# Two weight loads of a fused recurrence and expert kernel, moved and cut into other pieces

## The chip, the core and the metric

The kernel runs on one core of one Trainium2 chip. The metric is the device time of one execution in microseconds; smaller is better. The core has engines with instruction queues of their own: TensorE (PE, with its weight loads PEld), VectorE (DVE), ScalarE (ACT), GpSimd (POOL) and SyncE (SP). SP issues nearly all the transfers, in order; POOL issues the gathers and scatters by index. The transfers of both run on the same 16 DMA engines.

## The reference

Two stages follow each other. The first is a recurrence over 768 time steps for 4 batches and 8 heads of 48 channels:

```python
for t in range(S):
    cur = einsum('bhd,bhe->bhde', u * k[t], v[t])
    y[t] = einsum('bhd,bhde->bhe', r[t], state + cur)
    state = w[t][..., None] * state + einsum('bhd,bhe->bhde', k[t], v[t])
```

Its output, as 3072 tokens of 384 values, goes to a layer of 8 experts. A token whose product with `w_skip` is not positive is left as it is. The others go to the expert with the largest gate:

```python
h = maximum(x[mask] @ w1[e], 0)            # w1: 384 x 1024
out[mask] = x[mask] + gate[mask] * (h @ w2[e])   # w2: 1024 x 384
```

## The kernel before, in words

**The recurrence.** The work is cut into 24 chunks of 128 time steps (all heads of a batch at a time). The program's loop over `s` runs from -2 to 24. In step `s` it loads chunk `s + 4`, prepares chunk `s + 2` (two scans on DVE, lines 309 and 331, with the products `rk`, `kq` and `rp` on POOL), makes the scores and masks of chunk `s + 1` (`psA` on PE, `asb` on DVE), finishes chunk `s` (`outputs`, `evict`, `rows_out`), and stores chunk `s - 1` to `out` (line 435). So step `s` begins on DVE with the scan of chunk `s + 2`: step 5 at 37.88 us, step 12 at 73.22, step 16 at 94.47, step 21 at 121.09. The order on PE, ACT, DVE and POOL is as the program is written.

**The router.** After every six chunks a router runs, spread in small pieces over the following steps: gates, ranks, and marks (`hot`, on POOL, ACT or DVE). After the last six it gives the indices `idr`, by which POOL gathers the tokens of the experts (line 442). An early part of expert 0 (`early_expert`, 128 tokens, gathered by line 609) fills PE while the last router runs.

**The experts.** Matmuls of the experts 1 to 7 use split weights: a high part (an ACT copy to float32r) and a low part (raw less high). `w12` has both weights of an expert; `load_weights(e, q)` brings one of them (q = 0 the first, q = 1 the second; 1.5 MB) into a raw buffer. There are two raw buffers. `r0` takes (0, 0) and all later first weights but expert 1's; `r1` takes (0, 1), then (1, 0), then (1, 1), then the second weights of the others. A new load into a buffer waits for the last reader of what was in it. Expert 0's first weights are used raw. A weight is split in six slices of 512 columns, numbered 0 to 5 for the first weights and 6 to 11 for the second:

- `split_high(e, i)` (lines 101 to 108) makes the high part on ACT and puts the low part, a subtraction on POOL (line 107), on the list `low_parts`, which is run in the next step behind that step's `prep_reads`.
- `split_slice(e, i)` makes the high part on ACT (line 88) and the low part on DVE (line 89).

Before, (0, 1) is loaded in steps 5, 6 and 7, (1, 0) in 16, 17 and 18, (0, 0) in 19, 20 and 21, one transfer of 512 KB each. `parts` is the list of slices for `split_high`: expert 0's slices 6 to 11 from step 7 on, in steps in which no marks are waiting (7, 8, 12, 13, 14 and 15), expert 1's slice 0 in step 18 and its slices 1 to 5 from step 22 on, two per step.

**Behind the recurrence.** A loop runs the last router with pieces of `early_expert` between. Then come the rest of `early_expert`, `early_tokens(1)` (the next tokens of expert 0, transposed to `xT0[1]`), the gates and the indices `ids`, and `load_weights(1, 1)`, held back until the first gather has landed. Then `expert(e)` runs for all experts. In its loop over `q` it makes the hidden values `psH`, their high part `hh` (ACT) and low part `hl` (DVE), and one slice of the next expert's weights; then `tokens(e + 1)` makes `xTh` and `xTl`, then the outputs `psO` are made and scattered. `expert(0)` splits slices 6 to 11 of expert 1: those of `load_weights(1, 1)`.

Of the kernel before, what the change touches and what calls it, by code (L numbers as in the profile page):

```python
# [20 lines left out]
E, DM, DF = 8, 384, 1024  # L21
# [7 lines left out]
KC = DM // P  # L29
# [6 lines left out]
NHB = 11  # L36
HEAD = 7
STEP = 214
W_AT = 4
RW = 2112  # L40
R_OFF = 1 + NP * CW
K_OFF = R_OFF + NP * P
# [14 lines left out]
def rwkv_moe_kernel(ctx, tc, wrk, wrk0, vN, uP, wgs, wgp, w12, cst, out):  # L57
    nc = tc.nc
# [13 lines left out]
    def wtile(e, k):  # L72
        nm = f"{WN[k]}{e % 2}"
        pool = wset0 if nm in ("w1h1", "w1l1", "w2h0", "w2l0") else wset1[0]
        t = wsp[e, k] = pool.tile([P, KC * DF], F32R, tag=nm, name=f"{nm}_{e}")
        return t

    def load_weights(e, q):
        m = 1 if e == 1 else q
        wr = wset0.tile([P, KC * DF], F32, tag=f"r{m}", name=f"r{m}_{e}{q}")  # L80
        raws[e, q] = wr
        for i in range(3):
            o = i * 1024
            yield nc.sync.dma_start(wr[:, o:o + 1024],
                                    w12[e, :, q * KC * DF + o:q * KC * DF + o + 1024])

    def split(dst_h, dst_l, src, eng=None):
        nc.scalar.copy(dst_h, src)  # L88
        (eng or nc.vector).tensor_tensor(dst_l, src, dst_h.bitcast(F32), op=ALU.subtract)  # L89

    def split_slice(e, i, eng=None):
        q, cs = i // 6, slice((i % 6) * 512, (i % 6 + 1) * 512)
        for k in (2 * q, 2 * q + 1):
            if (e, k) not in wsp:
                wtile(e, k)
        split(wsp[e, 2 * q][:, cs], wsp[e, 2 * q + 1][:, cs], raws[e, q][:, cs], eng)
# [3 lines left out]
    def split_high(e, i):  # L100
        q, cs = i // 6, slice((i % 6) * 512, (i % 6 + 1) * 512)
        for k in (2 * q, 2 * q + 1):
            if (e, k) not in wsp:
                wtile(e, k)
        hi, lo, raw = wsp[e, 2 * q][:, cs], wsp[e, 2 * q + 1][:, cs], raws[e, q][:, cs]
        nc.scalar.copy(hi, raw)
        low_parts.append(lambda: nc.gpsimd.tensor_tensor(lo, raw, hi.bitcast(F32),
                                                         op=ALU.subtract))
# [31 lines left out]
    with tc.tile_pool(name="att", bufs=2) as att, \  # L140
# [141 lines left out]
        later, held, marks, ending = deque(), [], deque(), []  # L282
# [14 lines left out]
        work, lgs, gens = {}, {}, {}  # L297
# [327 lines left out]
        def early_tokens(j):  # L625
            ps = ps1.tile([P, KC, P], F32, tag="psT", name=f"psX0{j}", bufs=2)
            for kc in range(KC):
                nc.tensor.transpose(ps[:, kc], xg[j][:, kc * P:(kc + 1) * P], ident)
            nc.scalar.copy(xT0[j], ps)
# [3 lines left out]
        def early_low(k):  # L633
            while hfs and k > 0:
                dst, hf, hh = hfs.pop(0)
                nc.vector.tensor_tensor(dst, hf, hh, op=ALU.subtract)
                k -= 1
# [25 lines left out]
        def fill(k):  # L663
            psw = ps1.tile([P, 512], F32, tag="psT", name="psw", bufs=2)
            for _ in range(k):
                nc.tensor.matmul(psw, warm[:, :P], warm, start=True, stop=True)

        with tc.manual_schedule():
            setup()
            fill(FILL0)  # L670
            parts = [(4, 0, i) for i in range(6, 12)] + [(15, 1, 0)] + [(19, 1, i) for i in range(1, 6)]
            for s in range(-2, n + 1):
                on = lambda i: 0 <= i < n
                if s == -1:
                    for o in range(2):
                        for g in range(2):
                            at = 2 * (g ^ o)
                            nc.sync.dma_start(wgp_half[half(o), g, :, 2 * D:],
                                              wgp[half(g), at:at + 2, 2 * D:])
                if s + 4 < n:  # L680
                    load_chunk(s + 4)
                if on(s + 3) and s + 3 >= 1:
                    load_turned(s + 3)
                    load_v(s + 3)
                if s == 1:
                    nc.sync.dma_start(c_sb[:, C_IOTA:], cst[:, C_IOTA:])
                if s == LATE:
                    nc.sync.dma_start(wgs_sb, wgs)
                if on(s - 1):
                    store(s - 1)  # L690
                marked = len(marks)
                if pace[0] == 1:
                    mark_some()
                for i0, m in GROUPS:
                    if i0 + m == s:
                        pace[0] = 1 if i0 + m < LATE else 2
                        later.append(router(i0, m))
                        if i0 + m == LATE:
                            later.append(early())
                if on(s):  # L700
                    update(s)
                    if s == 0:
                        fill(3)
                if on(s + 2):
                    prep_scan(s + 2)
                drip(pace[0])
                if on(s):
                    outputs(s)
                if on(s + 2):
                    prep_keys(s + 2)  # L710
                    drip(pace[0])
                    prep_reads(s + 2)
                while low_parts:
                    low_parts.pop()()
                if s == -2:
                    bonus_keys(0)
                    nc.gpsimd.memset(vt_sb[3], 0.0)
                    nc.gpsimd.memset(onesb, 1.0)
                    nc.gpsimd.memset(ohs, 0.0)
                    nc.gpsimd.memset(key, 0.5)  # L720
                if on(s):
                    evict(s)
                    carry(s)
                if on(s + 1):
                    scores(s + 1)
                    bonus_sums(s + 1)
                    rows_of_keys(s + 1)
                    if s == -1:
                        fill(4)
                    flush()  # L730
                    mask(s + 1, 0)
                    mask(s + 1, 1)
                    bonus(s + 1)
                    drip(3 * pace[0])
                if on(s + 2):
                    prep_check(s + 2)
                if s == n - 1:
                    early_tokens(0)
                if on(s):
                    rows_out(s)  # L740
                flush(False)
                if pace[0] > 1:
                    mark_some(3)
                if s in (1, 2, 3):
                    nc.scalar.copy(*((trib, tri), (identb, ident),
                                     (iota, c_sb[:, C_IOTA:C_IOTA + 2 * P]))[s - 1])
                if s == 4:
                    nc.scalar.copy(toks_ps[:, :GROUPS[-1][1], :, 0], tok[:, GROUPS[-1][0]:])
                k = s + 1 - W_AT
                for eq, k0 in (((0, 1), 2), ((1, 0), 13), ((0, 0), 16)):  # L750
                    if k == k0:
                        gens[eq] = load_weights(*eq)
                    if k0 <= k < k0 + 3:
                        next(gens[eq])
                for _ in range(1 if s < 22 else 2):
                    if parts and k >= parts[0][0] and (not marked or s == 15):
                        split_high(*parts.pop(0)[1:])

        for p in parts:
            split_high(*p[1:])  # L760
        while low_parts:
            low_parts.pop()()
        while len(later) > 1:
# [5 lines left out]
        with tc.manual_schedule(engines={nc.tensor.engine, nc.scalar.engine, nc.vector.engine}):  # L769
            todo, due, done = early_expert(), HEAD * STEP, [0]  # L770
            while later:
                drip()
                flush()
                due += STEP
                while due > 0:
                    due -= next(todo, 1 << 20)
                    done[0] += 1
            early_low(1)
            for k in range(done[0], 6 * FC - 4):
                next(todo)  # L780
            early_tokens(1)
            ending.pop()()
            nc.vector.tensor_reduce(gates, pt[:, :, 2:].rearrange("p j q e -> p j e q"),
                                    axis=AX, op=ALU.add)
            nc.vector.tensor_scalar(idf, gates, 0.0, BIG, op0=ALU.is_equal, op1=ALU.mult)
            nc.vector.tensor_tensor(ids, idf, idr, op=ALU.add)
            drain(todo)
            held_back(load_weights(1, 1), gathered[0])
# [309 lines left out]
```

## Time and profile before

| | us |
|---|---|
| median of 3 runs | 287.21 |
| lowest and highest run | 287.07, 288.65 |
| the profiled execution | 286.06 |
| its span, first to last instruction | 284.2 |
| PE busy | 271.2 |
| DVE busy | 217.0 |
| ACT busy | 159.4 |
| POOL busy | 145.9 |

Busy time is the time in which an engine executes; the span is what the trace shows. The difference between the profiled execution's own time and its span, 1.86 us, lies around the instructions. All busy figures are sums over stages with different limits, and the rows further below go by stage.

### The profile page before, as it was taken

Reading aid. Unit: us, or ns where it says so; the run is one execution under the profiler, and the core shown is the slowest. Engines: PE = TensorE matmul, PEld = TensorE weight load, DVE = VectorE, ACT = ScalarE, POOL = GpSimd, SP = SyncE. Lnnn points to the kernel's source line nnn. Section 1 sums busy time; section 2 is a strip of 40 time slices with the busy share of each in tenths; the row PEclk is TensorE's granted clock in tenths of the full one; section 3 lists DMA queues with packets and bytes.
Section 4 is the critical chain, followed back from the end, with each engine's and each line's share of the span. In section 5 each row is a group of like instructions: output and inputs, shape, how many; then the busy total and the mean of one; then the engine's idle time right before and its main releaser. Section 6 shows DMA issues by size and latency. Waiting matters only on the chain.

```text
span 284.2 us, 8967 instructions
## 1 busy us (share of the span) xinstructions
PE 271.2 (95%) x3601; PEld 248.9 (88%) x3602; DVE 217.0 (76%) x414; ACT 159.4 (56%) x464; POOL 145.9 (51%) x140
## 2 busy tenths in 40 slices
PE   6998999999999999999999999999999999999993
PEld 2687878788887888887999999999999999999992
DVE  7997999999989999972747697948859588595320
ACT  5175555787658957768416573827638276381310
POOL 4986775699978998974656625011030110201111
PEclk9999999999999999999999999999999999999999
DMA  7999999998999869992078997565672656700001
GB/s 217 239 311 333 277 345 339 363 332 246 297 278 302 252 218 348 308 310 65 28 256 294 345 314 267 212 213 200 221 258 68 231 200 221 268 5 28 10 5 41
DMA packets 26131, 64.41 MB, mean 227 GB/s; under 512 B 4342, under 2 KB 15386, under 8 KB 26080
## 3 DMA queue, kind: packets, MB, share of 16 engines
q1 hardware_dynamic: 23712, 58.14, 62.3%
q0 software_dynamic: 2048, 5.48, 5.9%
q8 instruction: 30, 0.49, 0.7%
q10 hardware_dynamic: 320, 0.13, 0.2%
q14 instruction: 21, 0.17, 0.2%
HBM read 56.69 MB, written 7.86 MB: 227 GB/s over the span
## 4 chain that ended last, share of the span: by engine, by line
PE 57%; POOL 8%; issue 6%; DVE 4%; ACT 3%; DMA 1%; POOLq 0%; DVEq 0%; ACTq 0%
PE psH L884 7%; PE psH L883 7%; PE psH L882 7%; PE psO L906 6%; PE psO L908 6%; PE psO L907 6%; PE psH L133 4%; PE psY L409 3%; POOL rp L336 2%; PE psA L358 2%; POOL kq L326 2%; PE psY L413 2%; PE psX L815 2%; PE psO L658 2%; PE psX L425 1%
## 5 line engine op out<-in xcount | busy, mean ns | idle before, releaser
L820 POOL DMA_INDIRECT out<-fin,ids x16 | 16.8, 1047 | 99.1 <-DVE fin L915 92.7
L889 ACT ACTIVATE hh<-psH 128x256 fp32r<-128x256 f32 x60 | 23.1, 385 | 56.6 <-PE psH L884 53.4
L884 PE MATMUL psH<-xTh,w1l 128*128 128x256 f32 x168 | 47.5, 283 | 0.0
L883 PE MATMUL psH<-xTl,w1h 128*128 128x256 f32 x168 | 47.5, 283 | 0.0
L882 PE MATMUL psH<-xTh,w1h 128*128 128x256 f32 x168 | 47.5, 283 | 0.0
L906 PE MATMUL psO<-w2h,hh 128*128 128x384 f32 x120 | 40.9, 341 | 0.0
L908 PE MATMUL psO<-w2h,hl 128*128 128x384 f32 x120 | 40.2, 335 | 0.0
L907 PE MATMUL psO<-w2l,hh 128*128 128x384 f32 x120 | 40.1, 335 | 0.0
L894 DVE SCALAR_TENSOR_TENSOR hl<-psH,hh 128x256 fp32r<-128x256 f32 x60 | 25.1, 418 | 13.3 <-ACT hh L889 12.0
L326 POOL TENSOR_TENSOR kq<-wrk,q 128x512 f32<-128x512 f32 x24 | 28.2, 1177 | 11.7 <-DVE q L309 3.5
L364 DVE TENSOR_TENSOR asb<-psA,c_sb 128x512 f32<-128x512 f32 x48 | 30.4, 676 | 3.5 <-PE psA L358 3.4
L331 DVE TENSOR_TENSOR_SCAN rh<-wrk,rowsk,pss 128x520 f32<-128x520 f32 x24 | 31.1, 1296 | 2.0
L318 POOL TENSOR_TENSOR rk<-wrk 128x512 f32<-128x512 f32 x24 | 31.0, 1292 | 2.4 <-DMA wrk<-wrk 2.4
L884 PEld LDWEIGHTS psH<-xTh,w1l 128*128 128x128 f32 x168 | 32.2, 192 | 0.0
L883 PEld LDWEIGHTS psH<-xTl,w1h 128*128 128x128 f32 x168 | 32.2, 192 | 0.0
L882 PEld LDWEIGHTS psH<-xTh,w1h 128*128 128x128 f32 x168 | 32.2, 191 | 0.0
L309 DVE TENSOR_TENSOR_SCAN q<-wrk,pss 128x520 f32<-128x520 f32 x24 | 29.5, 1230 | 3.0 <-DMA wrk<-wrk 0.9
L336 POOL TENSOR_TENSOR rp<-wrk,rh 128x512 f32<-128x512 f32 x23 | 27.2, 1181 | 5.4 <-DVE rh L331 5.0
L89 DVE TENSOR_TENSOR w2l<-r,w2h 128x512 fp32r<-128x512 f32 x42 | 27.7, 685 | 2.0 <-ACT w2h L88 1.4
L409 PE MATMUL psY<-asb,v 128*48 128x128 f32 x384 | 26.5, 276 | 2.6 <-DVE psY L381 2.3
L915 DVE SCALAR_TENSOR_TENSOR fin<-psO,gates,xg 128x384 f32<-128x384 f32 x15 | 9.3, 618 | 25.2 <-PE psO L908 24.6
L358 PE MATMUL psA<-rp,kq 64*64 64x128 f32 (+1 forms) x768 | 26.0, 251 | 1.8 <-issue 1.1
(154 smaller groups left out, 608.4 us busy)
## 6 DMA issues: line engine op xcount, KB each, us to landing
r<-w SPq DMA_DIRECT2D x48, 512.0 KB
wrk<-wrk SPq DMA_DIRECT2D x21, 772.5 KB
v<-vN SPq DMA_DIRECT2D x24, 192.0 KB
vt<-wrk SPq DMA_DIRECT2D x48, 96.0 KB
out<-x SPq DMA_DIRECT2D x24, 192.0 KB
wrk<-wrk SPq DMA_DIRECT2D x1, 579.4 KB
wrk<-wrk SPq DMA_DIRECT2D x1, 512.0 KB
wrk<-wrk SPq DMA_DIRECT2D x1, 384.0 KB
```

Of the source, the lines that this page charges most:

```text
L318: nc.gpsimd.tensor_tensor(work[i]["rk"].rearrange("p a j -> p (a j)"), t[:, R_OFF:K_OFF], t[:, K_OFF:V_OFF], op=ALU.mult)
L326: nc.gpsimd.tensor_tensor(kq, wk["k"], wk["q"][:, :, 1:1 + P], op=ALU.mult)
L331: nc.vector.tensor_tensor_scan(rh.rearrange("p a j -> p (a j)"), wk["w"][:, 0:NP * CW], reads_at[:, :NP * CW], rowsk, op0=ALU.mult, op1=AL ...
L336: eng.tensor_tensor(rp, wk["r"], rh[:, :, :P], op=ALU.mult)
L358: nc.tensor.matmul(psa[g][j:j + HP, a, j:], wk["kq"][rows, a, j:j + HP], wk["rp"][rows, a, j:], start=True, stop=True)
L409: nc.tensor.matmul(y_at(a, g), v[:, 2 * a + g], wk["asb"][g][:, a], start=False, stop=True, skip_group_check=True)
L882: nc.tensor.matmul(ps, w1h[:, o:o + P], xTh[:, kc], start=(kc == 0), stop=False)
L883: nc.tensor.matmul(ps, w1h[:, o:o + P], xTl[:, kc], start=False, stop=False)
L884: nc.tensor.matmul(ps, w1l[:, o:o + P], xTh[:, kc], start=False, stop=(kc == KC - 1))
L906: nc.tensor.matmul(pso, h[j, fc][0], w2h[:, o], start=(fc == 0), stop=False)
L907: nc.tensor.matmul(pso, h[j, fc][0], w2l[:, o], start=False, stop=False)
L908: nc.tensor.matmul(pso, h[j, fc][1], w2h[:, o], start=False, stop=(fc == FC - 1))
```

## The change

`load_weights` makes six transfers of 256 KB (512 columns) instead of three of 512 KB, for every load of weights. A table `fetch` gives the step of each: (0, 1) one piece each in steps 5, 6, 8, 9, 13 and 15; (0, 0) two each in 19, 20 and 21; (1, 0) two each in 22, 23 and 24. A table `parts` gives the step of each `split_high`: expert 0's slices 6 to 11 in steps 7, 11, 12, 13, 18 and 21. Expert 1's slices 0 to 5 are no longer in it: they are split by `split_slice`, three ahead of the rest of `early_expert` and three behind `early_tokens(1)`. Both low parts of `early_expert` are made ahead of them.

```diff
-        for i in range(3):
-            o = i * 1024
-            yield nc.sync.dma_start(wr[:, o:o + 1024],
-                                    w12[e, :, q * KC * DF + o:q * KC * DF + o + 1024])
+        for i in range(6):
+            o = i * 512
+            yield nc.sync.dma_start(wr[:, o:o + 512],
+                                    w12[e, :, q * KC * DF + o:q * KC * DF + o + 512])
...
-            parts = [(4, 0, i) for i in range(6, 12)] + [(15, 1, 0)] + [(19, 1, i) for i in range(1, 6)]
+            fetch = {5: (0, 1), 6: (0, 1), 8: (0, 1), 9: (0, 1), 13: (0, 1), 15: (0, 1)}
+            fetch.update({t: (0, 0) for t in (19, 20, 21)})
+            fetch.update({t: (1, 0) for t in (22, 23, 24)})
+            parts = {t: 6 + i for i, t in enumerate((7, 11, 12, 13, 18, 21))}
...
-                k = s + 1 - W_AT
-                for eq, k0 in (((0, 1), 2), ((1, 0), 13), ((0, 0), 16)):
-                    if k == k0:
+                if s in fetch:
+                    eq = fetch[s]
+                    if eq not in gens:
                         gens[eq] = load_weights(*eq)
-                    if k0 <= k < k0 + 3:
+                    for _ in range(1 if eq == (0, 1) else 2):
                         next(gens[eq])
-                for _ in range(1 if s < 22 else 2):
-                    if parts and k >= parts[0][0] and (not marked or s == 15):
-                        split_high(*parts.pop(0)[1:])
-
-        for p in parts:
-            split_high(*p[1:])
+                if s in parts:
+                    split_high(0, parts[s])
...
-            early_low(1)
+            early_low(2)
+            for i in range(3):
+                split_slice(1, i)
             for k in range(done[0], 6 * FC - 4):
                 next(todo)
             early_tokens(1)
+            for i in range(3, 6):
+                split_slice(1, i)
             ending.pop()()
```

## Rows read from the trace of the kernel before

**Rows 1.** Windows: stretch, its length, busy us (x instructions) per engine, clock, DMA.

```profile
core 0: us, PE busy (x) PEld busy (x) DVE busy (x) ACT busy (x) POOL busy (x), PEclk, DMA share, GB/s
...
41.00:126.00 85.00, 81.78 (x1733) 70.90 (x1729) 80.67 (x149) 60.74 (x213) 74.84 (x67) 1.00 0.95 300
126.00:135.00 9.00, 8.36 (x145) 6.83 (x141) 2.40 (x9) 5.93 (x17) 4.14 (x5) 1.00 0.32 109
135.00:151.50 16.50, 16.49 (x157) 16.02 (x156) 10.12 (x34) 6.31 (x18) 9.78 (x9) 1.00 0.47 166
151.50:280.00 128.50, 127.83 (x909) 127.22 (x907) 87.41 (x174) 65.15 (x147) 25.91 (x24) 1.00 0.52 182
```

**Rows 2.** Timeline of DVE, steps 7 to 20: start, length, instruction, [idle before <-releaser].

```profile
54.10 1.24 DVE L309 TENSOR_TENSOR_SCAN q<-wrk,pss 128x520 f32<-128x520 f32 x1 [0.41 <-ACT gall L505]
...
106.64 1.29 DVE L331 TENSOR_TENSOR_SCAN rh<-wrk,rowsk,pss 128x520 f32<-128x520 f32 x1
107.85 1.26 DVE L364 TENSOR_TENSOR asb<-psA,c_sb 128x512 f32<-128x512 f32 x2
...
115.82 1.24 DVE L309 TENSOR_TENSOR_SCAN q<-wrk,pss 128x520 f32<-128x520 f32 x1 [0.17 <-ACT gall L505]
```

**Rows 3.** Timeline of POOL, steps 13, 17 and behind the recurrence.

```profile
80.69 1.18 POOL L326 TENSOR_TENSOR kq<-wrk,q 128x512 f32<-128x512 f32 x1 [1.37 <-DVE oh L476]
...
100.28 1.27 POOL L107 TENSOR_TENSOR w2l<-r,w2h 128x512 fp32r<-128x512 f32 x1
...
127.15 1.25 POOL L609 DMA_INDIRECT xg<-out,id  x1 [0.85 <-DMA r<-w]
...
140.57 1.02 POOL L442 DMA_INDIRECT xg<-out,idr  x1 [2.05 <-DVE pss L495]
```

**Rows 4.** Timeline of PE behind the recurrence.

```profile
134.33 2.42 PE L133 MATMUL psH<-xT,r 128*128 128x128 f32 x20
...
144.38 0.49 PE L628 MATMUL psX<-c_sb,xg 128*128 128x128 f32 x3
...
151.78 0.42 PE L906 MATMUL psO<-w2h,hh 128*128 128x384 f32 x1
...
156.15 0.28 PE L883 MATMUL psH<-xTl,w1h 128*128 128x256 f32 x1
```

**Rows 5.** Groups of instructions, the splits: busy us, mean ns of one.

```profile
L89 DVE TENSOR_TENSOR w1l<-r,w1h 128x512 fp32r<-128x512 f32 x36 | 24.9, 691 | 1.8 <-issue 0.2
...
L88 ACT CAST w1h<-r 128x512 fp32r<-128x512 f32 x36 | 22.2, 615 | 0.0
...
L107 POOL TENSOR_TENSOR w1l<-r,w1h 128x512 fp32r<-128x512 f32 x6 | 7.5, 1266 | 3.9 <-ACT lgs L432 3.3 <-ACT w1h L106 0.6
```

**Rows 6.** Timeline of SP's queue: transfers issued.

```profile
101.58 0.33 SPq L84 DMA_DIRECT2D r<-w  x1
...
126.26 9.29 SPq L435 DMA_DIRECT2D out<-x  x3
...
143.82 1.31 SPq L84 DMA_DIRECT2D r<-w  x3
```

**Rows 7.** Timeline of ACT behind the recurrence.

```profile
134.61 0.20 ACT L432 COPY lgs<-psX 128x36 f32<-128x36 f32 x1
...
142.16 0.21 ACT L574 CAST vals<-pss 128x6 bf16<-128x6 f32 x1
...
144.91 0.48 ACT L629 COPY xT<-psX 128x384 f32<-128x384 f32 x1 [2.54 <-PE psX L628]
...
149.12 0.62 ACT L88 CAST w2h<-r 128x512 fp32r<-128x512 f32 x1 [1.22 <-DMA r<-w]
```

**Rows 8.** Timeline of DVE behind the recurrence.

```profile
142.84 1.29 DVE L636 TENSOR_TENSOR h0l<-hf,h0h 128x512 fp32r<-128x512 f32 x2
...
153.22 1.01 DVE L89 TENSOR_TENSOR xTl<-psX,xTh 128x384 fp32r<-128x384 f32 x2
...
156.91 0.62 DVE L915 SCALAR_TENSOR_TENSOR fin<-psO,gates,xg 128x384 f32<-128x384 f32 x1 [1.49 <-PE psO L908]
```

**Rows 9.** DMA queues, 148.5 to 149.5 us: packets, MB, share of 16 engines.

```profile
q1 hardware_dynamic: 109, 0.39, 98.4%
```

More of the change, by code (lines that the diff above doesn't have):

```diff
@@ L38 @@
 STEP = 214
-W_AT = 4
 RW = 2112
@@ L690, in rwkv_moe_kernel @@
                     store(s - 1)
-                marked = len(marks)
                 if pace[0] == 1:
```

## The prediction

> **What bounds the kernel now.** I read the busy time by stage first [rows 1]. The recurrence, 41 to 126 us, keeps DVE at work for 80.67 of 85 us, PE for 81.78, POOL for 74.84, ACT for 60.74. DVE comes nearest to a real limit: its timeline shows one long row of instructions, with only five waits that have a name (first and last in [rows 2], the others 0.30, 0.41 and 0.30 us), 1.6 us together, all five behind the router's small steps, none behind a transfer or a weight split. The rest of its 4.3 idle us are gaps of under 0.1 us between two instructions. The chain of waits does name POOL for much of 86 to 106 us, but the timelines say that this is a tie: where PE's scores waited for POOL's `rp`, DVE took up the mask (107.85) as its own scan from 106.64 ended, so it lost nothing [rows 2]. POOL has a 1.27 us subtraction in such a step, and before one `kq` it waits 1.37 us for DVE [rows 3].
>
> From 134.33 on PE is the bound: 16.49 busy of 16.5 us, then 127.83 of 128.5 [rows 1, 4]. Whatever delays one of PE's inputs there comes out at the end one for one; whatever is done sooner is worth nothing unless PE's start at 134.33 moves.
>
> The profiled execution took 286.06 us, a span of 284.2 and 1.86 around it. The median of the runs, 287.21, is 1.15 above. I work out a difference against the profiled one and put it on the median.
>
> **Part 1: expert 0's second weights in pieces.** Three 512 KB transfers in steps 5 to 7 become six of 256 KB, and the six splits (an ACT copy of 0.62 us, a POOL subtraction of 1.27 one step later [rows 5]) move. POOL's subtractions for them ran in steps 8, 9, 13, 14, 15 and 16; they will run in 8, 12, 13, 14, 19 (in place of expert 1's first) and 22. So POOL gets back 1.27 us in each of steps 9, 15 and 16, and pays 1.27 in step 12, where the wait of 1.37 before `kq` at 80.69 covers it (uncovered, it would cost those 1.27). The new ACT copies in steps 11 and 21 go to an engine with 24 idle us. Each piece is issued two steps or more ahead of its copy. Since DVE was not waiting for POOL, ACT or DMA, I take 0 to 0.2 us of gain, 0.1. Bounds: a gain of at most DVE's named waits, 1.6 us; a loss of 1.27 if step 12's cover isn't there.
>
> **Part 2: SP's queue.** Expert 1's first weights leave steps 16 to 18. There SP stood at 101.58 until POOL's last subtraction (100.28 + 1.27) set the raw buffer free [rows 3, 6], with the loads of step 17 behind it; no consumer was late, so this is worth 0. The same wait comes back in step 22: the sixth part's subtraction stands on POOL behind the first gather, 127.15 + 1.25 = 128.40, so the buffer is free at 129.7. Behind SP's wait are the stores of chunks 22 and 23, the last of the three that went out between 126.26 and 135.55 as their data came [rows 6]. Held till 129.7, the earlier one would still be out 5 us ahead of the last, which waits for its data as before. So nothing gets late. Two 256 KB pieces go out then, two in step 23, two behind the last store, the last at 135.55 + 0.86 = 136.4.
>
> How long does a 256 KB piece take to land? The trace has none. One gather of 192 KB went out at 140.57 + 1.02 and released SP's load at 143.82: 2.2 us [rows 3, 6]. At the other end, the first 512 KB after it, amid gathers, went out at 143.82, and ACT's copy waited for it until 149.12: 5.3 us [rows 6, 7]. I take 2.8, near the gather, because the size is near and DMA is nearly empty in both places: the gather's 2.2, 0.17 for 64 KB more at 0.39 MB per us [rows 9], and 0.4 for other traffic. The last piece of expert 1's first weights then lands at 139.2 (141.7 at the slow end), and the first copy of it cannot start before 142.37. Covered.
>
> **Part 3: the splits behind the recurrence.** Five splits on ACT and POOL in 130 to 138.5 us go, and with step 18's all six come back as ACT copies and DVE subtractions. Taking ACT's copies out of the tail gives nothing: `lgs` at 134.61 [rows 7] waits for PE anyhow, and PE is at work on expert 0 by then. ACT: three copies from 142.37 at some 0.53 us from one to the next end at 144.0, before `xT` at 144.91 [rows 7]; three more run from 145.3 to 146.95. DVE: `h0l` ends at 144.13 [rows 8]; six subtractions, 0.69 us each [rows 5] and 0.61 from one to the next, end at 147.8. `gates`, `ids` and `fin` come behind them, at 147.8 to 149.1; `gates` are first used by DVE's `fin` at 156.91 [rows 8], and PE writes into their PSUM bank from 151.78 on [rows 4], so this is hidden.
>
> **Part 4: what is late next.** Expert 1's second weights (`load_weights(1, 1)`) use the same raw buffer. They left at 143.82; now they wait for the sixth subtraction and leave at 147.9, 4.1 us later. But `split_slice(1, 6)` needs the first 256 KB only: landed at 147.9 + 2.8 = 150.7, against 149.12. Behind this copy stand, on ACT and DVE, the next `hh` and `hl` and expert 1's `xTh`/`xTl`. Before, `xTl` ended at 153.22 + 1.01 = 154.23 [rows 8], 5.11 us behind the copy's start, a stretch in which DVE runs on from one to the next. Now: 150.7 + 5.1 = 155.8. PE wants it at 156.15 [rows 4]. So 1.9 us of slack are used up but for 0.35, and PE loses nothing: 0. At the slow end, 5.3 us, the copy starts at 153.2, `xTl` ends at 158.3, and PE stalls 2.2 us.
>
> Sum: −0.1 + 0 + 0 + 0, so 286.0 for the profiled one and 287.1 to 287.2 on the median: I say 287.2. A measurement of this kernel tells a change from none at about 0.5%, 1.4 us.
>
> **A rule of the Trainium skill.** In [rows 9] the load queue moves 0.39 MB in one us while several 512 KB transfers are in flight. "DMA: Bandwidth & Descriptors", section Bandwidth, says to batch transfers to 1 MiB or more for three quarters of peak; its fit (section Anatomy of one DMA) is about 2.0 us fixed and bytes/436e3. By that, an estimate, a piece takes 2.6 us and the first lands at 150.5: no change. If the fixed part came once per piece, one after another, it would be a loss; that is the third rival. The trace speaks against it: SP puts three out in 1.31 us without waiting [rows 6], and the queue is 98% busy.
>
> **The rivals.**
> *POOL sets the pace* (faster). For it: the chain through `kq`, `rp` and `w2l`, and 3.8 us given back in steps 9, 15, 16. Against: DVE is full. It can give no more than the named waits, 1.6 us: 285.6. Chance 0.13.
> *The first piece of expert 1's second weights is late* (slower). For it: SP leaves 4.1 us later, the slack left is 0.35. Against: fewer gathers in the way than at 144 to 149 us, half the size. It decides from a landing of 3.15 us; price up to 2.2 us: 289.4 at most. Chance 0.16, of which some two thirds over 1.4 us.
> *Pieces land one after another* (slower). For it: the queue's gaps are not known. At 2.8 each the fourth lands at 147.9 + 11.2 = 159.1; behind it copy, subtraction and `xTl`, 2.2 us: 161.3, a stall of 5.1: 292.3. Chance 0.03.
> *SP's new wait holds the last stores* (slower). The gather of 140.57 needs them landed, and its 192 KB are there 0.56 us before PE's transpose at 144.38 [rows 4, 6]. It decides if the buffer is free only after some 134.5; each us beyond is a us: 288.5 with one and a quarter. Chance 0.04.
>
> **How the numbers follow.** No change that can be told: 0.64, its own range 286.4 to 287.8. Faster by over 0.5%: the POOL rival's most, 0.12. Slower by over 0.5%: two thirds of the late piece and the other two, with a little for a loss in steps 11 and 12, 0.2. Same: 0.68, with the milder parts of the rivals. The range goes from the first bound, 285.6, to the late piece's price, 289.4.
>
> **What would show it.** The pace of steps 8 to 21 unchanged, with DVE's named waits still about 1.6 us; POOL idle in steps 15 and 16; SP's first piece of expert 1 out at about 129.7; DVE's sixth subtraction done at 147.8 and SP's next load then; ACT's copy `w2h` starting at 150.7; PE without a gap before its first `xTl` matmul. The forecast is wrong if that copy starts after 152.5, if a store or gather slips past 144.4, or if the scans come in shorter steps.

## The result, and the profile after

| | before | changed |
|---|---|---|
| median of 6 runs each, us | 287.19 | 290.50 |
| lowest and highest, us | 287.02, 288.65 | 289.65, 291.24 |
| the profiled execution, us | 286.06 | 291.24 |
| its span, us | 284.2 | 289.4 |

The ratio is 1.0108, with an interval from 1.0076 to 1.0140: the change costs about 3 us, where none was forecast, and 290.50 lies above the 289.4 at which the prediction's range ends. Ratios, here and below, leave out runs more than 1.5% above their kernel's fastest one, and medians are of all runs, so a ratio need not be the quotient of two medians. The stages of the profiled executions, in us, say where it goes. Both kernels were profiled once more as experiments (below), and those executions have columns too. The stages are cut by the scans of steps 5 and 21 on DVE, the first matmul of expert 0's early hidden values, the first transposes of expert 1's tokens, the first matmul with their `xTl`, the first transposes of expert 2's tokens, the start of the last scatter, and the end of the span.

| stage | before | before again | changed | changed again |
|---|---|---|---|---|
| start to scan of step 5 | 37.88 | 37.75 | 40.01 | 38.00 |
| to scan of step 21 | 83.21 | 83.24 | 82.91 | 82.88 |
| to early hidden values | 13.24 | 13.25 | 13.24 | 13.27 |
| to transposes of expert 1 | 16.88 | 16.88 | 16.53 | 16.51 |
| to first matmul with `xTl` | 4.94 | 4.94 | 6.52 | 6.66 |
| to transposes of expert 2 | 8.51 | 12.23 | 8.60 | 10.00 |
| to the last scatter | 115.60 | 115.61 | 115.60 | 115.60 |
| to the end of the span | 3.94 | 3.90 | 5.99 | 5.38 |

The first row differs by 2.0 us between two executions of the changed kernel, so it is chance and no part of the change. The sixth row differs by 3.7 us between two executions of the kernel before; I come back to it. Four rows differ by the change: 0.3 and 0.35 us gained in the recurrence and in the last router (the second and the fourth row), 1.6 to 1.7 lost at the passage from expert 0 to expert 1 (the fifth row, called the stall or the first loss below), 1.4 to 2.1 lost behind the last scatter (the second loss). Together that is a loss of 2.98 us for the first pair of profiles and of 2.47 for the second.

The windows of the changed kernel, with the columns of [rows 1]:

```profile
41.00:126.00 85.00, 81.63 (x1762) 70.85 (x1757) 80.67 (x148) 59.04 (x206) 72.58 (x65) 1.00 0.91 286
...
135.00:152.70 17.70, 17.51 (x167) 17.29 (x168) 11.22 (x36) 7.97 (x21) 5.65 (x5) 1.00 0.52 153
152.70:167.80 15.10, 14.40 (x104) 13.29 (x103) 12.91 (x25) 10.78 (x25) 11.10 (x10) 1.00 1.00 355
167.80:283.40 115.60, 114.68 (x810) 114.08 (x808) 77.05 (x153) 56.91 (x127) 16.16 (x15) 1.00 0.49 165
```

DVE is as busy in the recurrence as before, 80.67 us. From 152.7 to 167.8 PE and PEld, which were full before (13.50 of 13.50 us from 151.2 to 164.7), have idle time, and the DMA engines have none: share 1.00 at 355 GB/s, where it was 0.94 at 321. That is the stretch in which the loss falls.

**The place of the first loss.** SP's queue, then ACT, DVE and PE of the changed kernel between the experts (its line numbers are up to two off those of before):

```profile
131.64 0.80 SPq L83 DMA_DIRECT2D r<-w  x2
...
149.34 0.33 SPq L83 DMA_DIRECT2D r<-w  x1
```

```profile
152.25 0.62 ACT L87 CAST w2h<-r 128x512 fp32r<-128x512 f32 x1 [2.87 <-DMA r<-w]
...
154.53 0.62 ACT L87 CAST w2h<-r 128x512 fp32r<-128x512 f32 x1 [1.37 <-DMA r<-w]
...
155.94 0.62 ACT L87 CAST w2h<-r 128x512 fp32r<-128x512 f32 x1 [0.52 <-DMA r<-w]
...
156.74 0.61 ACT L87 CAST w2h<-r 128x512 fp32r<-128x512 f32 x1
```

```profile
145.52 3.79 DVE L88 TENSOR_TENSOR w1l<-r,w1h 128x512 fp32r<-128x512 f32 x6
...
158.14 1.02 DVE L88 TENSOR_TENSOR xTl<-psX,xTh 128x384 fp32r<-128x384 f32 x2
```

```profile
152.69 0.82 PE L817 MATMUL psX<-c_sb,xg 128*128 128x128 f32 x6
...
156.26 0.44 PE L910 MATMUL psO<-w2h,hl 128*128 128x384 f32 x1 [0.16 <-DVE hl L896]
...
159.21 0.39 PE L885 MATMUL psH<-xTl,w1h 128*128 128x256 f32 x1 [0.45 <-DVE xTl L88]
```

DVE's six subtractions end at 149.31, and SP's next load goes out at 149.34. The first piece is there for ACT at 152.25, 2.9 us later. Before, the copies behind the first one ([rows 7] show the first) ran on without a wait:

```profile
149.92 0.61 ACT L88 CAST w2h<-r 128x512 fp32r<-128x512 f32 x1
...
150.93 0.62 ACT L88 CAST w2h<-r 128x512 fp32r<-128x512 f32 x1
```

Now the second waits 1.37 us for its piece and the third 0.52. These 1.89 us are nearly all that `xTl` is later behind the first copy: it ends 6.91 us behind that copy's start, where it was 5.11, 1.80 more. Counted from PE's first transpose (152.69, before 151.21) the first copy itself starts 1.65 us later. Of these 3.45 us, 1.92 were slack before (from 154.23, where `xTl` ended, to 156.15, where PE took it up). That leaves 1.53 of the 1.58 us in the table. PE's named wait is only 0.45 us; the rest is spread over matmuls of `psO` that start late in small amounts, as `hh` and `hl` of the same chain come late.

What the DMA engines did from 151 to 156 us (packets, MB, share of 16 engines):

```profile
q1 hardware_dynamic: 603, 1.10, 68.1%
q0 software_dynamic: 64, 0.20, 26.8%
```

The gathers (q0) took over a quarter of the engines' time for 0.20 MB, the loads (q1) two and a half times as much for 1.10 MB. Per byte the gathers took more than twice as much here. How much of the second and third piece's lateness is due to them was not tried.

**The place of the second loss.** What SP waits for in the last 7 us, first the changed kernel, then late512, an experiment below with 512 KB transfers for the later experts:

```profile
SPq L1096 <- DMA out<-fin,ids: 17.3, 2, 14.1
SPq L1096 <- PEq L1096: 2.6, 2, 2.1
```

```profile
SPq L1098 <- DMA out<-fin,ids: 17.4, 2, 14.2
SPq L1098 <- PEq L1098: 0.7, 2, 0.5
```

The last wait on PE's queue is 2.1 us in place of 0.5. PE's last matmul is the same 0.9 us ahead of the last scatter in both. On q14, the queue that the page calls instruction, both kernels have a packet some 3 us and another 3.5 us behind the last scatter's start. The changed kernel has a third one at 5.6 us, and so have two later executions, after_again (5.1) and own_buffer (5.4); in each of the three the span ends 0.3 us behind it, and SP's long wait is on PE's queue.

**The place of a gain.** Six `hot` of the last router on DVE before (the first by itself, then all six), POOL beside them before, and the six after:

```profile
137.58 1.02 DVE L528 TENSOR_SCALAR hot<-iota,rall 128x256 bf16<-128x256 bf16 x1
```

```profile
137.58 2.00 DVE L528 TENSOR_SCALAR hot<-iota,rall 128x256 bf16<-128x256 bf16 x6
```

```profile
134.80 3.73 POOL L107 TENSOR_TENSOR w1l<-r,w1h 128x512 fp32r<-128x512 f32 x3 [0.59 <-ACT w1h L106]
```

```profile
139.32 1.27 DVE L527 TENSOR_SCALAR hot<-iota,rall 128x256 bf16<-128x256 bf16 x6
```

The same six instructions take 0.73 us less when POOL has no subtraction beside them, and the first one is all of it: 1.02 us where the others take 0.27. It ends at 138.60, just behind POOL's last subtraction (138.53). Two experiments below bear this out: in hold_only, with POOL's subtractions as before, the first `hot` takes 1.03 us and the router's stage 16.89; in two_behind, where POOL's last subtraction ends at 135.21, ahead of `hot` at 137.16, the six take 1.27 us and the stage 16.53.

### The profile page after: what moved, and what is told of

Its sections match the earlier page's. It is cut to its first block, busy times and chain, and to the rows that moved or that the text cites. A ratio compares the mean times of both kernels' runs of the same rounds, so it can differ in the third digit from the quotient of the medians.

```text
span 289.4 us, 9048 instructions
## 1 busy us (share of the span) xinstructions
PE 271.8 (94%) x3602; PEld 249.6 (86%) x3602; DVE 220.7 (76%) x420; ACT 160.3 (55%) x464; POOL 139.1 (48%) x134
## 4 chain that ended last, share of the span: by engine, by line
issue 34%; POOL 8%; PE 5%; DMA 4%; DVE 2%; ACT 2%; POOLq 1%; SPq 0%; DVEq 0%; ACTq 0%
POOL out L822 5%; DMA xg<-out,idr 2%; DMA r<-w 2%; POOL xg L441 2%; PE psH L132 2%; PE psY L408 1%; DVE w1l L88 1%; PE psA L357 1%; PE psY L412 1%; ACT w2h L87 1%; POOLq L924 0%; POOL kq L325 0%; POOL rp L335 0%; PE psX L424 0%; ACT xTh L87 0%
## 5 line engine op out<-in xcount | busy, mean ns | idle before, releaser
L88 DVE TENSOR_TENSOR w1l<-r,w1h 128x512 fp32r<-128x512 f32 x42 | 28.7, 692 | 2.1
```

## The experiments

All times are medians; each kernel has its batch's runs of the kernel before beside it.

**1. Both kernels again, unchanged.** What of the difference between two profiles is chance?

> The kernel before, unchanged. Of the 5.2 us between the two profiled spans, 2.1 arise in the first five steps (the scan of chunk 7 starts at 40.01 against 37.88 us) and 2.0 behind the last scatter, where the change edits nothing. Theory A, these are chance from one execution to the next: this profile shows the scan of chunk 7 anywhere from 37.9 to 40, and the ratio is 1.00 within 0.5%. Theory B, they belong to the changed program: chunk 7 at 37.9 within 0.3 again and the span's end some 3 us behind the last scatter.

> The changed kernel, unchanged. Theory A (chance): ratio about 1.01 as measured, but the scan of chunk 7 and the end behind the last scatter fall elsewhere than 40.0 and 5.0 us. Theory B (the program): chunk 7 at 40.0 within 0.3 and 5 us at the end again. Both: from the scan of chunk 7 to the end of PE's last matmul it is 1.0 us longer than in the kernel before (0.65 gained up to the first transposes of expert 1's tokens, 1.7 lost behind them).

Measured: the kernel before 287.24 (ratio 0.9994, 0.9972 to 1.0015), the changed one 290.01 (1.0108, 1.0039 to 1.0176), with 287.25 for the batch's runs of before. So the time of the start was chance (37.75 and 38.00); the loss of some 3 us was not. The two columns "again" above are these executions.

The sixth row of the table showed another thing, in the kernel before itself. ACT and PE of before_again:

```profile
162.56 0.38 ACT L889 ACTIVATE hh<-psH 128x256 fp32r<-128x256 f32 x1 [3.48 <-PE psH L884]
```

```profile
163.45 0.39 PE L882 MATMUL psH<-xTh,w1h 128*128 128x256 f32 x1 [1.96 <-DVE hl L894]
```

ACT stood for 3.48 us and PE then waited for `hl`. Behind these 2 us without a matmul the granted clock of 163 to 170 us was 0.76 in place of 1.00, a mean between its two levels, 1.2 and 2.4 GHz. PE's `psH`, named as the releaser, was long done. The same gap is in profiles of pad_unrun and after_again, and in some others there is none, so it is one source of the spread between executions (285.91 to 288.15 for the batch's runs of before) and not of this change. Its cause was not settled.

**2. A buffer of its own for the first two late pieces.** If the stall comes from waiting for the raw buffer, pieces 1 and 2 of `load_weights(1, 1)` should not wait.

```diff
+        own = wset0.tile([P, 1024], F32, tag="r2", name="r2") if (e, q) == (1, 1) else None
...
-            yield nc.sync.dma_start(wr[:, o:o + 512],
+            yield nc.sync.dma_start((wr if own is None or i > 1 else own)[:, o:o + 512],
```

> The changed kernel with a raw buffer of its own for the first two 256 KB pieces of expert 1's second weights, so that they need not wait for the six subtractions behind the recurrence. Theory 1 (the late reload of the raw buffer costs 1.7 us): these two leave at about 145.3 (on the changed kernel's clock) instead of 149.3, ACT's first copy of them starts by 150.6 instead of 152.25, PE's wait of 1.7 us before the first matmuls of expert 1 goes nearly whole, and the time falls by 1.2 to 1.7 us. Rival (those 1.7 us come from the order on DVE, six subtractions ahead of hl): the wait stays and the time is that of the changed kernel within 0.4 us.

Measured: 288.99 (1.0057, 1.0026 to 1.0087). ACT's copies:

```profile
147.79 0.61 ACT L90 CAST w2h<-r 128x512 fp32r<-128x512 f32 x1
...
155.38 0.62 ACT L90 CAST w2h<-r 128x512 fp32r<-128x512 f32 x1 [2.77 <-DMA r<-w]
```

The first copy no longer waits, but the fourth stands 2.77 us: pieces 3 to 6 still wait for the subtractions and go out from 147.87 on. From the transposes to `xTl` it is 6.51 us, as in the changed kernel. So the first piece, on which the prediction set its eye, is not what decides. The median is 1.0 us below the changed kernel's 290.01 all the same; the profile shows no stage that gave it (5.66 us lie behind the last scatter), the two intervals overlap, and it stays unexplained.

**3. Only the smaller transfers.** The kernel before, with 256 KB pieces everywhere, two at each place of one.

```diff
-        for i in range(3):
+        for i in range(6):
...
                         next(gens[eq])
+                        next(gens[eq])
```

> The kernel before with all weight loads in 256 KB pieces, two issued where one of 512 KB was. Theory 1 (the moved splits cost, the piece size does not): 287.2 within 0.7 us. Rival (pieces of half the size are dearer in the queue, 24 KB per engine more often, and this is the loss): 289 to 290.5 us, with ACT's first copy of expert 1's second weights later than 149.1.

Measured: 289.81 (1.0096, 1.0065 to 1.0127). The pieces alone cost as much as the whole change, but in other places. Chunk 23's scan is late for its input:

```profile
122.95 1.24 DVE L309 TENSOR_TENSOR_SCAN q<-wrk,pss 128x520 f32<-128x520 f32 x1 [1.36 <-DMA wrk<-wrk]
```

So step 21 begins 1.4 us later than before, counted from step 5: SP issued this input at 115.39 and not at 110.82. As the program's instructions show, SP's transfers signal on eight semaphores in turn, and each waits for the one eight before it; with pieces of half the size, eight transfers are half the bytes. That this is what held SP back is argued from there and not tried by itself. (A piece of 256 KB is 16 KB for each of 16 engines; the 24 KB of the expectation is wrong.) Further 1.2 us lie behind the last scatter (5.11 in place of 3.94), and there too SP's long wait is 1.5 us on DVE's queue and q14 has no third packet. The changed kernel spreads its pieces over other steps, and its recurrence has no such loss.

**4. The two halves of the change by themselves, with 512 KB elsewhere.** part1 has (0, 1) in six pieces in steps 5 to 12 and all else as before; part23 has (1, 0) loaded in steps 22 to 24 and split behind the recurrence, all of 512 KB.

```diff
part1:
+        n_ = 6 if (e, q) == (0, 1) else 3
...
+                if s in (5, 6, 8, 9, 10, 12):
...
+                    next(gens[0, 1])
...
part23:
-            parts = [(4, 0, i) for i in range(6, 12)] + [(15, 1, 0)] + [(19, 1, i) for i in range(1, 6)]
+            parts = [(4, 0, i) for i in range(6, 12)] + []
-                for eq, k0 in (((0, 1), 2), ((1, 0), 13), ((0, 0), 16)):
+                for eq, k0 in (((0, 1), 2), ((1, 0), 19), ((0, 0), 16)):
...
+            for i in range(3):
+                split_slice(1, i)
...
```

> The kernel before, with only expert 0's second weights in six 256 KB transfers in steps 5 to 12; all other loads of 512 KB, all splits at the steps of before. Both theories put the stall between experts 0 and 1 elsewhere, so 4.94 us there. If 256 KB pieces cost by themselves (each waits for the eighth transfer before it), six of them early cost little: 287.2, within 0.5 of before. If three more transfers already lengthen the program's end, the time from the last scatter to the end is over 5 us, and the time 288.5.

> The kernel before, with only the second half of the change: expert 1's first weights are loaded in steps 22 to 24 and split behind the recurrence, in 512 KB transfers as before. Theory A (the stall between experts 0 and 1 comes from loading expert 1's second weights late, with whatever transfer size): the first transposes of expert 1's tokens to the first matmul with their xTl takes about 6.5 us, not 4.94, the router phase (early hidden layer to those transposes) 16.5 and not 16.9 us, the last scatter still ends the span by 3.9 us: 288.4 in all. Theory B (the stall is made by the 256 KB pieces): 4.94 us, 286.9 in all.

Measured, beside 287.19: part1 287.06 (0.9997, 0.9956 to 1.0037), part23 290.43 (1.0087, 1.0048 to 1.0126). The stall belongs to the second half, and it does not need small pieces. ACT of part23:

```profile
153.28 0.62 ACT L88 CAST w2h<-r 128x512 fp32r<-128x512 f32 x1 [4.18 <-DMA r<-w]
...
156.48 0.62 ACT L88 CAST w2h<-r 128x512 fp32r<-128x512 f32 x1 [1.50 <-DMA r<-w]
```

With 512 KB the first copy waits longer than with 256 KB (4.18 against 2.87), and from the transposes to `xTl` it is 7.33 us, not the 6.5 expected (this execution took 291.78; hold_only below has the same waits in one of 288.95). That does not show that smaller pieces help: late512 below loads (1, 1) in 256 KB pieces too, and has 7.50. The router took 16.51 us, so its gain also belongs to this half; behind the last scatter it is 3.96.

**5. The end: fewer pieces, and a longer program that isn't run.** late512 is the changed kernel with 512 KB from expert 2 on; pad_unrun is the kernel before with more transfers in the branch that isn't taken.

```diff
late512:
-        for i in range(6):
+        n_ = 6 if e < 2 else 3
...
+        for i in range(n_):
pad_unrun:
-                nc.sync.dma_start(w1, w12[e, :, :KC * DF])
-                nc.sync.dma_start(w2, w12[e, :, KC * DF:])
+                for i in range(4):
...
+                    nc.sync.dma_start(w1[:, o:o + 768], w12[e, :, o:o + 768])
+                    nc.sync.dma_start(w2[:, o:o + 768], w12[e, :, KC * DF + o:KC * DF + o + 768])
```

> The changed kernel, with the loads of experts 2 and later in three transfers of 512 KB again, six of 256 KB for experts 0 and 1 alone. Theory A (about 1.6 us of the loss is the stall at expert 1, and 1.2 to 2 us lie behind the last scatter, since the program of SP is longer): the stall stays at 6.5 us, the time behind the last scatter goes back to 3.9 us, 288.6 in all. Theory B (the small pieces of the later experts cost in the loop itself): the loop of experts 2 to 7 gets shorter than 88.5 us, and the end stays at 5.4 or above. Rival C (neither): 290.

> The kernel before, with 6 more transfers for each expert in the branch that is never taken with these inputs, so that the program is longer and nothing more is executed. If a longer program costs at its end, the time from the last scatter to the end goes from 3.9 us to 5 us or more, 288.5 in all. If only executed transfers count, 3.9 us and 287.2.

Measured, beside 287.19: late512 289.12 (1.0065, 1.0029 to 1.0101), pad_unrun 287.14 (1.0006, 0.9962 to 1.0050). late512 has 4.1 us behind the last scatter and keeps the stall, 7.50 us from transposes to `xTl`; the second loss is gone and the first stays. pad_unrun has 4.06 (its profiled execution took 290.69, above its median, with ACT's gap of experiment 1): instructions that aren't executed cost nothing there. late512 also shows the gain of the recurrence alone: the scans of chunks 12 and 13 lie 4.54 us apart, 4.72 before and in part1. PE's `psA` starts at 65.28 there and at 65.46 before, and `asb` on DVE comes 0.16 us sooner (66.41 and 66.57). POOL has a subtraction in that step in the kernel before and in part1, and none in late512: the moved splits give it and not the pieces.

**6. The stall made in the kernel before, and taken out with the splits still behind the recurrence.** hold_only puts two dummy additions behind `fin0` and lets the loads of (1, 1) wait for the second. two_behind moves only the last two splits.

```diff
hold_only:
...
+            nc.vector.tensor_tensor(dum, fin0, xg[0], op=ALU.add)
+            held.append(nc.vector.tensor_tensor(dum, dum, xg[0], op=ALU.add))
...
-            held_back(load_weights(1, 1), gathered[0])
+            held_back(load_weights(1, 1), held[0])
two_behind:
-            parts = ... + [(19, 1, i) for i in range(1, 6)]
+            parts = ... + [(19, 1, i) for i in range(1, 4)]
...
-            early_low(1)
+            early_low(2)
+            split_slice(1, 4)
+            split_slice(1, 5)
```

> The kernel before, with nothing of the change; two dummy additions of 0.6 us are put behind fin0 on DVE, and the loads of expert 1's second weights wait for the second one, so that they are issued near 147.9 and not at 143.8 us. Theory A (the late issue of these loads alone makes the stall): from the first transposes of expert 1's tokens to the first matmul with xTl 6.5 to 7.5 us, not 4.94; 3.9 us behind the last scatter; 288.8 to 289.6 in all. Theory B (the stall comes from what the change puts on DVE and ACT in the tail): 4.94 us and 287.2.

> The kernel before, with the last two of the six splits of expert 1's first weights moved behind the recurrence, and no load moved, all of 512 KB. Theory A (what costs is that the loads of the second weights wait for all of the first ones' subtractions): with two subtractions behind the recurrence they end near 145.4, the loads go 1.6 us later than before and land in time, 4.94 us from the transposes to xTl, and the router phase keeps a part of the 0.35 us: 286.9 to 287.2 in all. Theory B (any split in the tail costs): 288 or more.

Measured, beside 286.66: hold_only 289.53 (1.0094, 1.0059 to 1.0130), two_behind 286.45 (0.9989, 0.9963 to 1.0016). hold_only on SP (the three loads of (1, 1) go out first), ACT and PE:

```profile
148.40 4.93 SPq L84 DMA_DIRECT2D r<-w  x6
```

```profile
152.51 0.62 ACT L88 CAST w2h<-r 128x512 fp32r<-128x512 f32 x1 [4.14 <-DMA r<-w]
...
155.63 0.62 ACT L88 CAST w2h<-r 128x512 fp32r<-128x512 f32 x1 [1.42 <-DMA r<-w]
```

```profile
158.89 0.38 PE L887 MATMUL psH<-xTl,w1h 128*128 128x256 f32 x1 [0.43 <-DVE xTl L89]
```

The late issue alone makes the stall: 7.20 us from transposes to `xTl`, with the copies at the same waits as in part23, without any split moved. The two additions hold up nothing else: `hl` behind them starts 0.41 us behind the start of its `hh` (148.00), as before (0.42). Of the 2.9 us in the medians the profile shows 2.3 there. In two_behind the loads go out at 144.72, counted from step 21's scan 1.2 us later than before (23.97 and 22.73 us behind it). The copies behind the first run on, it is 4.95 us to `xTl`, and the router takes 16.53 us.

**7. The second loss made in the kernel before.** pieces_late has 256 KB for experts 2 to 7 alone, two_late 768 KB for experts 3 to 7.

```diff
-        for i in range(3):
+        n_ = 6 if e >= 2 else 3        # two_late: 2 if e >= 3 else 3
+        for i in range(n_):
```

> The kernel before, with 256 KB transfers for experts 2 to 7 alone. Theory A (the longer program of executed transfers costs one more instruction fetch behind the last scatter): recurrence, router phase and the stall as before, from the last scatter to the end 5 to 6 us, not 3.9; 288.3 to 289.2 in all. Theory B (the end depends on what the first part of the program does): 3.9 us and 287.2.

> The kernel before, with the weights of experts 3 to 7 in two transfers of 768 KB in place of three of 512 KB, 10 transfers fewer. By the theory of the end (the length of the executed program decides when its last instructions are fetched) the time behind the last scatter is 3.9 us or less; the first slice of each weight waits for 768 KB and not 512, which the loads' lead in the loop hides: 286.8 to 287.3 in all. Rival: the larger first transfer makes the splits wait, the loop of experts 2 to 7 over 89 us, 288 or more.

Measured, beside 286.66: pieces_late 288.15 (1.0053, 1.0027 to 1.0078), two_late 286.78 (0.9992, 0.9970 to 1.0014). In pieces_late recurrence, router and stall are as before, and 4.95 us lie behind the last scatter. SP's waits there name another engine's queue:

```profile
SPq L1096 <- DVEq L1096: 1.3, 1, 1.3
SPq L1096 <- PEq L1096: 0.4, 2, 0.3
```

So the wait sits on PE's queue in one kernel and on DVE's in another, with no work of theirs before it. Of the 1.5 us in the medians the profile, of the shortest of its runs (286.45), shows 1.0 at the end. Fewer transfers than before gain nothing: 4.07 in two_late.

**8. Are the gains worth anything without the losses, and what does the end go by?** both_gains is two_behind with expert 0's splits in steps 7 and 10 to 14; two_behind_5 is two_behind again. pieces_2to4 and pieces_5to7 have 256 KB for three experts each.

```diff
both_gains:
-            parts = [(4, 0, i) for i in range(6, 12)] + [(15, 1, 0)] + ...
+            early_at = {t: 6 + i for i, t in enumerate((7, 10, 11, 12, 13, 14))}
+            parts = [(15, 1, 0)] + ...
...
pieces_2to4, pieces_5to7:
+        n_ = 6 if 2 <= e < 5 else 3     # and: 6 if e >= 5 else 3
```

> two_behind, with expert 0's splits in steps 7, 10, 11, 12, 13 and 14 in place of 7, 8, 12, 13, 14 and 15, so that POOL has no subtraction in steps 9 and 16; all loads of 512 KB at the steps of before. If the gains found so far are real and add up, the scans of chunks 12 to 13 and 18 to 19 come 4.55 us apart and not 4.72, the router phase takes 16.5 and not 16.88, no stall, 3.9 us at the end: 0.3 + 0.35 us below before, a ratio of 0.998, 286.4 beside 287.1. Rival: the new subtraction in steps 11 and 12, in which marks are made, costs as much as it gives: only the 0.35, ratio 0.999.

> two_behind again, with more rounds, for the interval: the 0.35 us of the router phase is a ratio of 0.9988; if the time of the end or of later stages gives it back, 1.000.

> The kernel before, with 256 KB pieces for experts 2 to 4 alone: 66 transfers of weights. If the loss behind the last scatter goes by the number, this and pieces_5to7 show the same time from the last scatter to the end, 3.9 to 4.2 (no loss yet) or about 5. If it goes by the place, only one of the two is near 5 or more.

> The kernel before, with 256 KB pieces for experts 5 to 7 alone: also 66 transfers. By number: as pieces_2to4. By place, with late transfers as the cause: 5 us or more here and 3.9 to 4.2 there.

Measured, beside 286.75: both_gains 287.09 (1.0004, 0.9974 to 1.0033), two_behind_5 287.18 (1.0024, 0.9992 to 1.0055). No version is shown to beat the kernel before. The router's gain is in all of their profiles (16.5 us), and in both_gains chunks 12 and 13 lie 4.54 us apart, though 18 and 19 still 4.71. The time is given back at the same place as ever; ACT of two_behind_5:

```profile
149.28 0.62 ACT L88 CAST w2h<-r 128x512 fp32r<-128x512 f32 x1 [1.75 <-DMA r<-w]
150.08 0.61 ACT L88 CAST w2h<-r 128x512 fp32r<-128x512 f32 x1
153.90 0.62 ACT L88 CAST w2h<-r 128x512 fp32r<-128x512 f32 x1 [2.92 <-DMA r<-w]
```

In this execution the second transfer landed 2.9 us after it was wanted, and it is 6.31 us to `xTl` (5.92 in both_gains, 4.95 in the profile of experiment 6). The loads went out 23.97 us behind step 21's scan here, as in the profile of experiment 6: the same 1.2 us of lateness cost nothing in one execution and 1.4 in the other. pieces_2to4 took 286.12 and pieces_5to7 286.92, one run each, with 3.9 and 3.85 us behind the last scatter: with 66 weight transfers the end is as before, wherever the pieces stand; with 84 (pieces_late) and 96 it costs. So the second loss goes with the number of transfers executed and begins between 66 and 84. Why it begins there stays open. The third packet on q14, 0.3 us ahead of the end in the three executions that have it, suggests that an engine's last instructions are fetched late, but pieces_late and pieces_only pay 1.0 and 1.2 us without a third packet. With more transfers the other engines' programs get more instructions too, those that wait for them; the runs do not tell the two apart.

## Why the prediction was wrong

It said 287.2 and no change. The sum's terms were −0.1, 0, 0 and 0; they measured −0.3, 0, −0.35 and +1.6, and a term of +1.4 to +2.1 was missing.

*Part 1* had the sign right and the size low: 0.3 us in place of 0.1, above its 0 to 0.2. Twice, at 66.57 and at 97.38, DVE's `asb` began some 0.06 us behind the end of its scan; without POOL's subtraction it began 0.09 ahead of it, 0.15 us each time. That is no named wait, and I had looked at the named waits alone. (I also misread those: of the five, the timeline puts one, at 84.91, down to a transfer of `v`, and two name no releaser.) The rival that POOL sets the pace was right by 0.3 us and no more.

*Part 2* held. SP's first piece of (1, 0) went out at 131.64; 129.7 with this profile's shift of 1.8 us (2.13 later at step 5, 0.3 gained since) is 131.5. No store and no gather was late: the stage to the early hidden values took 13.24 us in both.

*Part 3* had the ends of the work right: the six subtractions ended at 149.31, and 147.8 with the shift less the router's gain is 149.3. "Taking ACT's copies out of the tail gives nothing" looked at the wrong engine. Five subtractions left POOL too, and beside the last one DVE's six `hot` had taken 2.00 us in place of 1.27. These 0.73 us cover the 0.35 that the stage gained.

*Part 4* is the step that failed, in the sentence that `xTl` follows the copy by 5.11 us, "a stretch in which DVE runs on from one to the next". The release (149.34) and the landing of the first piece (2.9 us, 2.8 forecast) came as said. The first copy, too, started 1.65 us later, where 1.6 was forecast. But the 5.11 us were read from an execution in which the load was 5.3 us old by the first copy and every later slice was there when ACT came to it, though not all had landed: q1 still moved 0.36 MB from 149 to 150 us and 0.08 in the next two. Issued 4.0 us later, the first piece is wanted at once and the second and third come 2.3 and 1.4 us behind each other, beside gathers. So `xTl` ends 6.91 us behind the first copy. own_buffer shows that an early first piece doesn't help, hold_only that the late issue alone is enough. The rival of the late piece had the place and nearly the price (up to 2.2 us, 1.6 measured), but decided by the first piece alone, whose landing stayed under its 3.15 us. The rival of pieces one after another had the mechanism in part; its price, 5.1, took every piece at the full landing time.

*The missing term.* Nothing in the prediction looks behind the last scatter. late512 and pieces_late take the loss away and make it.

*The rule on batches.* The Trainium skill's page "DMA: Bandwidth & Descriptors", section Bandwidth, asks for larger transfers, and smaller ones did cost: pieces_only 2.6 us. But the rate didn't fall, as that section would have it: between the experts, with the DMA engines full (share 1.00), the changed kernel moved 355 GB/s, part23 347 and hold_only 368, both with 512 KB. The cost came from an input issued late (experiment 3) and from the end. The prediction's estimate of 2.6 us for a piece took a fit that the same page of the Trainium skill gives for transfers issued by GpSimd; these are SP's, and the first took 2.9.

## What to carry to other kernels

When a transfer is issued later, ask for each of its pieces when its consumer wants it; that the first one lands in time says nothing of the second, and a distance "consumer behind first copy" is only good while every later piece is there before its turn. A buffer that two loads share ties the second load to the slowest reader of the first: to move the reader is to move the load. Look at the last microseconds of the span as a stage of its own when a change adds executed instructions.

## What the runs showed of the hardware

DVE's bf16 `hot` instructions (128x256) took 2.00 us for six when the first began beside a POOL subtraction, and 1.27 without; that first one took 1.02 us and ended 0.07 us behind the subtraction. The Trainium skill's page "SBUF — State Buffer", section "SBUF: two separate sides", says that DVE and GpSimd share a pair of ports, which one instruction holds to its end; the trace agrees, in these two instructions and again in hold_only (1.03 us). ACT stood for 3.48 us with its inputs done while the DMA engines were full (share 1.00, 160 to 163 us of before_again), in some executions of either kernel. Behind the last scatter, 84 or 96 weight transfers took 4.95 to 5.99 us where 38 to 66 took 3.85 to 4.19, in waits of SP on the queues of engines that had no work left; why is open.
